# Loading queries and keys two tokens side by side in a partition, in an attention + two-MoE kernel

## The chip, the cores and the metric

The kernel runs on 1 core of one Trainium2 chip. The metric is the device time of one execution in microseconds (us), the median of several runs. The engines are named as in the profile: PE is the matmul engine (TensorE), PEld its weight loads, DVE is VectorE, ACT is ScalarE, POOL is GpSimd, and SP is the engine whose queue issues the DMAs here.

## What is computed

Windowed attention with a distance bias, then a soft mixture of experts, then a second mixture whose gate is balanced eight times. The change lies in the attention alone: how q and k get into the layout that the score matmul needs.

```python
# q, k, v: 4 batches x 8 heads x 576 tokens x 64, f32; window 128
scores = (q @ k.T) / 8 + slope[h] * -(i - j)      where 0 <= i - j < 128, else -1e9
attn   = softmax(scores);  x = (attn @ v) -> 2304 x 512
x = moe(x, phi, w1, w2)            # 8 experts, 4 slots each, 512 -> 1024 -> 512
x = moe2(x, w_gate, m1, m2)        # all 8 experts on every row; gate P from 8 rounds of row/column sums
```

## The kernel before, in words

**Stages.** The attention runs from the start to about 163 us. The soft mixture (`mm1`, line 764, and the loop at 839) runs to about 213 us. The second mixture, with its long row of f16 matmuls (lines 962 and 1034), fills the rest. Weights come in over SP's queue in all stages: during the attention the eight `w1` (`load_part`, line 57, 512 KB pieces) and `w2` of expert 0.

**Half-steps.** The attention works on two batches at a time (`j` = 0, 1) and on chunks of 64 queries, 9 chunks to a batch pair: 18 *tokens* `t` in the kernel's words. Each `t` is done in two half-steps of four heads, `s = 2 t + hf`, 36 in all. One trip of the loop at line 469 emits for half-step `s`: the DMAs, the scores of `s` (`emit_qk`, PE, then `emit_sm` on DVE), the normalization of `s-1` (`emit_nm`, DVE), the transposes of the weights of `s-2` (`emit_pt`, PE, copied out by ACT), the exponentials of `s` (`emit_exp`, ACT), the transposes that turn the next q and k (`emit_tr`), and the weighted sum of v for `s-3` (`emit_pv`, PE). `turned` then adds the transposes of a finished chunk (`emit_x`), and after every fourth chunk a generator (`group`, line 339) does the logits of the soft mixture, a piece per half-step. The schedule is manual: each engine and SP's queue run in the order in which the program emits.

**q and k.** `load_nat(t)` (line 126) loads chunk `t` of k and of q, two chunks ahead, into one tile each: 64 tokens of batch `j` = 0 on partitions 0 to 63, those of `j` = 1 on 64 to 127. One contiguous run in DRAM is one token of one head, 64 floats, 256 bytes. The second batch has neighbouring heads exchanged, so it takes two DMAs; a chunk takes six. The tiles have two buffers each. `emit_tr(t, "k")` makes four 128x128 transposes into one PSUM tile (pool `ps_t`, three buffers) in the first half-step of `t-1`, and DVE copies them into `kT` (line 156), a ring of four chunks; ACT copies some a second time (line 158) so that a window that wraps is contiguous. `emit_tr(t, "q")` makes two transposes in each half-step and DVE copies them into `qT` (line 160).

**Buffers that the change touches.** `xn` (line 273) holds up to five turned chunks for the sums of a group; `lt` and `lg` (lines 345 and 354) are small tiles of a group.

Of the kernel before, what the change touches and what calls it, by code (L numbers as in the profile page):

```python
# [8 lines left out]
F32 = mybir.dt.float32  # L9
# [15 lines left out]
def tile_kernel(ctx: ExitStack, tc: tile.TileContext, q, k, v, phi, w1, w2, w_gate, m1, m2, rel, out):  # L25
# [69 lines left out]
    with tc.manual_schedule():  # L95
        with ExitStack() as ab:
# [5 lines left out]
            with ExitStack() as at:  # L102
                nat = at.enter_context(tc.tile_pool(name="nat", bufs=2))
# [17 lines left out]
                qT = one.tile([128, 4, 2, 64], F32, name="qT")  # L121
# [4 lines left out]
                def load_nat(t):  # L126
                    bp, c = divmod(t, NCH)
                    for nm, src in (("k", k), ("q", q)):
                        nt_ = nat.tile([128, H, D], F32, tag=nm + "n", name=nm + "n")
                        nc.sync.dma_start(out=nt_[0:CH], in_=src[2 * bp, :, CH * c:CH * c + CH, :].rearrange("h i d -> i h d"))  # L130
                        heads = src[2 * bp + 1, :, CH * c:CH * c + CH, :].rearrange("(g a) i d -> i g a d", a=2)
                        turned_ = nt_[CH:].rearrange("p (g a) d -> p g a d", a=2)
                        for a in range(2):
                            nc.sync.dma_start(out=turned_[:, :, 1 - a, :], in_=heads[:, :, a, :])
                        natt[nm, t] = nt_
# [11 lines left out]
                def emit_tr(t, nm, gs=range(4)):  # L147
                    src = natt[nm, t]
                    ps = ps_t.tile([128, 4, 128], F32, tag="pt", name="pt")
                    for i, g in enumerate(gs):  # L150
                        nc.tensor.transpose(
                            ps[:, i, :], src[:, 2 * g:2 * g + 2, :].rearrange("p a d -> p (a d)"), idn)
                    pv_ = ps[:, 0:len(gs), :].rearrange("p g (j i) -> p g j i", j=2)
                    if nm == "k":
                        sl_ = t % 4
                        nc.vector.tensor_copy(out=kT[:, :, :, CH * sl_:CH * sl_ + CH], in_=pv_)
                        if sl_ < 2 and t >= 4:
                            nc.scalar.copy(out=kT[:, :, :, CH * (sl_ + 4):CH * (sl_ + 5)], in_=pv_)
                    else:
                        nc.vector.tensor_copy(out=qT[:, gs[0]:gs[-1] + 1], in_=pv_)  # L160
# [8 lines left out]
                def emit_qk(s):  # L169
                    t, hf = divmod(s, 2)  # L170
                    c = t % NCH
                    nch = min(c, 2) + 1
                    k0 = CH * ((t - nch + 1) % 4)
                    k1 = k0 + CH * nch
                    col = 192 - (k1 - k0)

                    ps = [ps_s.tile([128, 2, 256], F32, tag="s", name="s") for _ in range(2)]
                    for gg in range(2):
                        g = 2 * hf + gg
                        for j in range(2):  # L180
                            for a in range(2):
                                r0, c0 = CH * (a ^ j), CH * a
                                nc.tensor.matmul(ps[j][c0:c0 + CH, gg, col:192], lhsT=qT[r0:r0 + CH, g, j, :],  # L183
                                                 rhs=kT[r0:r0 + CH, g, j, k0:k1], start=True, stop=True,
                                                 tile_position=(r0, c0))
                    sc[s] = (ps, col)
# [82 lines left out]
                def emit_x(t):  # L269
# [3 lines left out]
                    xn[t] = sp.tile([128, DM], F32, tag="xn", name="xn", bufs=5)  # L273
# [65 lines left out]
                def group(g):  # L339
# [14 lines left out]
                    lg = sp.tile([128, 128], F32, tag="lg", name="lg", bufs=1)  # L354
# [20 lines left out]
                def group_end():  # L375
# [16 lines left out]
                    lg = sp.tile([128, 128], F32, tag="lg", name="lg", bufs=1)  # L392
# [40 lines left out]
                load_nat(0)  # L433
                nc.sync.dma_start(out=rel_sb[:, 3, :], in_=rel)
                load_nat(1)
# [5 lines left out]
                emit_tr(0, "k")  # L441
# [3 lines left out]
                emit_tr(0, "q", range(0, 2))  # L445
                emit_tr(0, "q", range(2, 4))

                NST = 2 * NT
                pre = [("w1", e, (wraw, wraw, wone, wpre, wpre, wpre, wpre, wcv)[e], p, 4) for e in range(NPRE) for p in range(4)]
# [8 lines left out]
                def turned():  # L458
                    while px:
                        t3 = px.pop(0)  # L460
                        if t3 < NT - 1:
                            emit_x(t3)
                        if t3 == NT - 1:
                            side.append(group_end())
                        elif t3 % 4 == 3:
                            side.append(group(t3 // 4))

                s = 0
                while s < NST + 4 or side or px:
                    t, hf = divmod(s, 2)  # L470
                    if s < NST:
                        if hf == 0:
# [12 lines left out]
                    if s < NST:  # L485
                        emit_exp(s)
                        if t + 1 < NT and hf == 0:
                            emit_tr(t + 1, "k")
                    if 3 <= s and s - 3 < NST:
                        emit_pv(s - 3)  # L490
                    if s < NST and t + 1 < NT:
                        emit_tr(t + 1, "q", range(2 * hf, 2 * hf + 2))
                    turned()
                    if 3 <= s and s - 3 < NST:
                        t3, hf3 = divmod(s - 3, 2)
                        if hf3 == 1:
                            emit_xt(t3)
                            px.append(t3)
# [730 lines left out]
```

## Time and profile before

| | |
|---|---|
| time, median of 3 runs | 973.59 us (971.21 to 976.7) |
| profiled execution, its own time | 977.32 us |
| its span, first to last instruction | 975.5 us |
| PE busy in the span | 940.9 us (96%) |
| DVE, ACT, POOL busy | 741.7, 611.8, 540.2 us |
| DMA packets under 512 B | 64240 of 95077 |

The span is the profiled time less 1.8 us around it. The profile counts an engine as busy while an instruction runs on it; a wait shows as the idle time in front of an instruction, with the one that ended it. In a timeline row the first number is the start, the second the length, both in us; `xN` means N instructions merged into one row; f32 matmuls count twice there. A timeline on SP shows the issue of a DMA, not its landing.

### The profile page before, as it was taken

The numbers are of one execution on the slowest core, as the hardware profiler recorded it, in microseconds if no ns is written. First come the engines' busy times: TensorE is split into PE (matmuls) and PEld (weight loads), VectorE is DVE, ScalarE is ACT, GpSimd is POOL, SyncE is SP. The second block draws the span as 40 slices with busy tenths as digits, with TensorE's granted clock in tenths as the row PEclk, the third lists the DMA queues.
The fourth block names the chain that finished last, engine by engine and source line by source line (L and its number), as shares of the span: only waits on it lengthen the run. The fifth ranks groups of instructions, "written<-read, shape, count | busy, mean of one in ns | idle before, by whom it ended". The sixth has DMA issues, their size and how long they took to land.

```text
span 975.5 us, 24588 instructions
## 1 busy us (share of the span) xinstructions
PE 940.9 (96%) x9629; PEld 790.9 (81%) x9629; DVE 741.7 (76%) x1920; ACT 611.8 (63%) x1493; POOL 540.2 (55%) x620
## 2 busy tenths in 40 slices
PE   8999999979899999999999999999999999999997
PEld 6676666437788888888888888888888888888886
DVE  5898886675996787777777777877787778777775
ACT  4777764646577677766666665666476656664442
POOL 0000000213488569857893897498658956995442
PEclk7999999999999999999999999999999999999999
DMA  6999999980200220032004001300220020001212
GB/s 132 241 236 227 237 269 329 365 311 2 98 2 1 94 92 2 1 101 85 1 2 164 22 1 57 129 2 2 89 97 1 2 94 6 1 2 34 55 44 66
DMA packets 95077, 90.13 MB, mean 92 GB/s; under 512 B 64240, under 2 KB 68208, under 8 KB 94960
## 3 DMA queue, kind: packets, MB, share of 16 engines
q1 hardware_dynamic: 94960, 88.55, 31.8%
q8 instruction: 76, 1.25, 0.5%
q14 instruction: 41, 0.34, 0.1%
HBM read 81.97 MB, written 4.72 MB: 89 GB/s over the span
## 4 chain that ended last, share of the span: by engine, by line
PE 69%; DVE 0%; issue 0%
PE x L1034 35%; PE y L1034 27%; PE z L962 6%; PE m L667 1%; PE m L542 0%; DVE ops L975 0%; DVE acc L1048 0%; DVE acc L1046 0%; PE m L925 0%
## 5 line engine op out<-in xcount | busy, mean ns | idle before, releaser
L1034 PEld LDWEIGHTS <-ops 128*128 128x128 f16 x6048 | 592.2, 98 | 73.8 <-issue 1.5
L994 POOL TENSOR_TENSOR ops<-s,ops 128x512 f16<-128x512 f32 x287 | 332.5, 1160 | 228.4 <-ACT ops L991 227.0
L1034 PE MATMUL x<-w2h,ops 128*128 128x256 f16 x2304 | 413.6, 273 | 2.2 <-ACT ops L972 0.7
L1034 PE MATMUL y<-w2h,ops 128*128 128x256 f16 x1728 | 319.5, 273 | 0.4 <-ACT ops L991 0.2
L1034 PE MATMUL x<-w2l,ops 128*128 128x256 f16 x1152 | 313.6, 273 | 0.0
L991 ACT CAST ops<-s 128x512 f16<-128x512 f32 x288 | 177.7, 617 | 216.0 <-DVE s L987 213.9
L1034 PE MATMUL y<-w2l,ops 128*128 128x256 f16 x864 | 235.6, 273 | 0.0
L1048 DVE SCALAR_TENSOR_TENSOR acc<-x,pe,acc 128x256 f32<-128x256 f32 x252 | 121.7, 483 | 77.5 <-PE x L1034 76.1
L972 ACT ACTIVATE ops<-z 128x512 f16<-128x512 f32 x216 | 128.6, 596 | 35.7 <-PE z L962 33.2
L975 DVE SCALAR_TENSOR_TENSOR ops<-z,ops 128x512 f16<-128x512 f32 x216 | 146.9, 680 | 0.0
L1048 DVE SCALAR_TENSOR_TENSOR acc<-y,pe,acc 128x256 f32<-128x256 f32 x189 | 91.3, 483 | 58.3 <-PE y L1034 57.9
L625 POOL TENSOR_TENSOR w2l<-w,w2h 128x256 f16<-128x256 f32 x168 | 112.7, 675 | 0.0
L987 DVE SCALAR_TENSOR_TENSOR s<-z,r 128x512 f32<-128x512 f32 x144 | 98.2, 682 | 11.3 <-ACT r L983 7.2
L987 DVE SCALAR_TENSOR_TENSOR s<-z,s 128x512 f32<-128x512 f32 x144 | 98.2, 682 | 6.5 <-ACT ops L972 6.3
L962 PE MATMUL z<-ct,stk 128*128 128x256 f16 x576 | 86.3, 273 | 4.5 <-DVE ops L975 3.8
L758 POOL MEMSET hz<- 128x480 f32 x2 | 1.0, 498 | 159.6 <-PE xp L258 158.4
L628 ACT CAST w2h<-w 128x256 f16<-128x256 f32 x168 | 67.3, 401 | 0.1
L962 PEld LDWEIGHTS <-stk 128*128 128x128 f16 x576 | 55.5, 98 | 14.3 <-DVE ops L975 4.8
L212 ACT ACTIVATE et<-et,mx 128x192 f32<-128x192 f32 (+2 forms) x144 | 61.2, 433 | 3.5 <-DVE mx L203 3.5
L203 DVE CUSTOM_DVE_ANT_0 et<-s,rel_sb 128x192 f32<-128x192 f32 (+2 forms) x144 | 39.5, 331 | 10.3 <-PE s L183 10.2
L258 PE MATMUL xp<-ptt,v 64*64 64x64 f32 (+1 forms) x1024 | 45.5, 244 | 1.5 <-DVE cn L328 0.5
L234 ACT COPY ptt<-pt 128x384 f32<-128x384 f32 (+2 forms) x72 | 28.6, 445 | 28.7 <-PE pt L233 28.6
(191 smaller groups left out, 917.7 us busy)
## 6 DMA issues: line engine op xcount, KB each, us to landing
w<-in_moe_w_dram SPq DMA_DIRECT2D x68, 512.0 KB, 7.3
w<-in_moe_w_dram SPq DMA_DIRECT2D x14, 2048.0 KB, 8.3
v<-in_v_dram SPq DMA_DIRECT2D x18, 256.0 KB, 4.8
out_dram<-acc SPq DMA_DIRECT2D x34, 128.0 KB, 2.4
kn<-in_k_dram SPq DMA_DIRECT2D x18, 128.0 KB, 6.2
kn<-in_k_dram SPq DMA_DIRECT2D x36, 64.0 KB, 5.3
qn<-in_q_dram SPq DMA_DIRECT2D x18, 128.0 KB, 5.4
qn<-in_q_dram SPq DMA_DIRECT2D x36, 64.0 KB, 4.8
```

The costliest lines, as they stand in the source:

```text
L212: nc.scalar.activation(out=runs[hh], in_=runs[hh], func=AF.Exp, bias=mx[:, hh:hh + 1], scale=-1.0, accum_out=sm[:, hh:hh + 1])
L258: nc.tensor.matmul(xp[j][64 * a:64 * a + 64, g, :], lhsT=vt[bp, vc, j][r0:r1, 2 * g + a, :], rhs=ptt[r0:r1, gg, 128 * blk + 64 * a:128 * b ...
L625: nc.gpsimd.tensor_tensor(out=out_, in0=x_, in1=y_, op=ALU.subtract)
L628: nc.scalar.copy(out=hi[:, i, r], in_=src[:, r])
L962: nc.tensor.matmul(ps[:, i], lhsT=stk[e][:, 128 * ft:128 * ft + 128], rhs=ct.rearrange("p (a n) t -> p a n t", a=2)[:, :, n, :], start=Tru ...
L972: nc.scalar.activation(out=ops_[m][:, k_, 0], in_=zb(m, i, j), func=AF.Relu)
L975: nc.vector.scalar_tensor_tensor(out=ops_[m][:, k_, 1], in0=zb(m, i, j), scalar=0.0, in1=ops_[m][:, k_, 0], op0=ALU.max, op1=ALU.subtract)
L987: nc.vector.scalar_tensor_tensor(out=new_sum(m, nm), in0=zb(m, i, j), scalar=0.0, in1=o, op0=ALU.max, op1=op)
L991: nc.scalar.copy(out=ops_[m][:, k_, 0], in_=sm_[m, nm])
L994: eng.tensor_tensor(out=ops_[m][:, k_, 1], in0=sm_[m, nm], in1=ops_[m][:, k_, 0], op=ALU.subtract)
L1034: nc.tensor.matmul(out_, lhsT=a_[:, k_, l_, i, :], rhs=r_[:, k_, i, :], start=(first and j == 0), stop=(j == 11), skip_group_check=True)
L1048: nc.vector.scalar_tensor_tensor(out=o, in0=ps, scalar=pe_[e][:, t:t + 1], in1=o, op0=ALU.mult, op1=ALU.add)
```

## The change

A *unit* is two neighbouring chunks of a batch pair (one chunk at the end, as there are nine), ten units in all. A tile now holds one unit's 128 tokens of both batches for four heads: partition `p` has tokens `2p` and `2p+1` side by side, so one contiguous run in DRAM is two tokens of one head, 128 floats, 512 bytes. After the landing, POOL exchanges the two middle blocks of 64 columns through a tile `swap` with three copies, so that a block of 128 columns holds one token of two heads. Four transposes turn a tile; the copies into `kT` and `qT` then write every second column. `qT` holds both chunks of a unit. q and k share one tag with four buffers, the tiles of one unit. `w1` comes in 1 MB pieces in every second half-step. `xn` has four buffers, and every fourth chunk is turned a half-step later; `lg` takes the buffer of `lt`.

```diff
-                nat = at.enter_context(tc.tile_pool(name="nat", bufs=2))
+                nat = at.enter_context(tc.tile_pool(name="nat", bufs=4))
-                qT = one.tile([128, 4, 2, 64], F32, name="qT")
+                qT = one.tile([128, 4, 2, 2 * CH], F32, name="qT")
+                swap = one.tile([128, 2, D], F32, name="swap")
-                def load_nat(t):
-                    bp, c = divmod(t, NCH)
-                    for nm, src in (("k", k), ("q", q)):
-                        nt_ = nat.tile([128, H, D], F32, tag=nm + "n", name=nm + "n")
...
+                units = [(bp, c, min(2, NCH - c)) for bp in range(2) for c in range(0, NCH, 2)]
+                wanted = [(u, nm, hf) for u in range(len(units)) for hf in range(2) for nm in "kq"]
+                def load_nat():
+                    if not wanted:
+                        return
+                    u, nm, hf = wanted.pop(0)
+                    bp, c, n = units[u]
+                    src = {"k": k, "q": q}[nm]
+                    nt_ = nat.tile([128, 2, 4, D], F32, tag="n", name=nm + "n")
+                    r1 = 32 * n
+                    for j in range(2):
+                        rows = nt_[r1 * j:r1 * j + r1].rearrange("p g (x r) d -> p g x (r d)", r=2)
+                        heads = src[2 * bp + j, 4 * hf:4 * hf + 4, CH * c:CH * (c + n), :].rearrange(
+                            "(g x) (p r) d -> p g x (r d)", x=2, r=2)
+                        if j == 0:
+                            nc.sync.dma_start(out=rows.rearrange("p g x e -> p (g x) e"),
+                                              in_=heads.rearrange("p g x e -> p (g x) e"))
+                        else:
+                            for x in range(2):
+                                nc.sync.dma_start(out=rows[:, :, 1 - x, :], in_=heads[:, :, x, :])
+                    all_ = nt_[0:2 * r1]
+                    nc.gpsimd.tensor_copy(out=swap[0:2 * r1], in_=all_[:, :, 1, :])
+                    nc.gpsimd.tensor_copy(out=all_[:, :, 1, :], in_=all_[:, :, 2, :])
+                    nc.gpsimd.tensor_copy(out=all_[:, :, 2, :], in_=swap[0:2 * r1])
+                    natt[u, nm, hf] = nt_
...
+                def emit_tr(u, nm, hf):
+                    bp, c, n = units[u]
+                    w = CH * n
+                    src = natt.pop((u, nm, hf))
+                    ps = ps_t.tile([128, 512], F32, tag="pt", name="pt")
+                    for i in range(4):
+                        r, g = divmod(i, 2)
+                        nc.tensor.transpose(ps[:, w * i:w * i + w],
+                                            src[0:w, g, 2 * r:2 * r + 2, :].rearrange("p x d -> p (x d)"), idn[0:w, 0:w])
+                    pv_ = ps[:, 0:4 * w].rearrange("q (r m p) -> q r m p", r=2, p=w // 2)
+                    def place(x_, o):
+                        return x_[:, 2 * hf:2 * hf + 2, :, o:o + w].rearrange("q g j (p r) -> q r (g j) p", r=2)
                     if nm == "k":
+                        nc.vector.tensor_copy(out=place(kT, CH * (c % 4)), in_=pv_)
+                        if c and c % 4 == 0:
+                            nc.scalar.copy(out=place(kT, CH * 4), in_=pv_)
                     else:
+                        nc.vector.tensor_copy(out=place(qT, 0), in_=pv_)
...
-                    xn[t] = sp.tile([128, DM], F32, tag="xn", name="xn", bufs=5)
+                    xn[t] = sp.tile([128, DM], F32, tag="xn", name="xn", bufs=4)
-                    lg = sp.tile([128, 128], F32, tag="lg", name="lg", bufs=1)
+                    lg = sp.tile([128, 128], F32, tag="lt", name="lg", bufs=1)
...
-                emit_tr(0, "q", range(0, 2))
-                emit_tr(0, "q", range(2, 4))
+                emit_tr(0, "q", 0)
+                for _ in range(2):
+                    load_nat()
+                for nm in "kq":
+                    emit_tr(0, nm, 1)
+                for _ in range(2):
+                    load_nat()
...
-                        if hf == 0:
-                            if t + 2 < NT:
-                                load_nat(t + 2)
-                        if s > 2 and pre:
+                        if s > 2 and s % 2 and pre:
                             load_part(*pre.pop(0))
...
-                        if t + 1 < NT and hf == 0:
-                            emit_tr(t + 1, "k")
+                        u = next((i for i, x_ in enumerate(units) if NCH * x_[0] + x_[1] == t + 1), None)
+                        if u is not None:
+                            emit_tr(u, "k", hf)
...
-                    if s < NST and t + 1 < NT:
-                        emit_tr(t + 1, "q", range(2 * hf, 2 * hf + 2))
+                    if s < NST and u is not None:
+                        emit_tr(u, "q", hf)
+                        for _ in range(2):
+                            load_nat()
...
-                            px.append(t3)
+                            px.append((s + 2 * (t3 % 4 == 0), t3))
```

**What moves on PE at the start of the program.** `pt<-idn,kn` and `pt<-idn,qn` are the transposes of k and q, `s<-kT,qT` the scores, eight to a half-step. Before (lines 151, 183):

```order
L83 MATMUL warm<-idn 128x128 x8
L151 MATMUL pt<-idn,kn 128x128 x4
L83 MATMUL warm<-idn 128x128 x3
L151 MATMUL pt<-idn,qn 128x128 x4
L183 MATMUL s<-kT,qT 64x64 x8
L151 MATMUL pt<-idn,kn 128x128 x4
L151 MATMUL pt<-idn,qn 128x128 x2
L183 MATMUL s<-kT,qT 64x64 x8
```

Changed (174 is the transpose, 210 the scores):

```order
L83 MATMUL warm<-idn 128x128 x8
L174 MATMUL pt<-idn,kn 128x128 x4
L83 MATMUL warm<-idn 128x128 x3
L174 MATMUL pt<-idn,qn 128x128 x4
L174 MATMUL pt<-idn,kn 128x128 x4
L174 MATMUL pt<-idn,qn 128x128 x4
L210 MATMUL s<-kT,qT 64x64 x16
L210 MATMUL s<-kT,qT 64x128 x8
```

The first scores now stand behind all four tiles of the first unit, where they stood behind one chunk of k and of q.

**What moves on SP's queue, from the first v to the first w1.** 130, 134 are loads of k and q, 144 of v, 64 of w1. Before:

```order
L144 DMA v<-in_v_dram 128x8x64
L144 DMA v<-in_v_dram 64x8x64
L130 DMA kn<-in_k_dram 64x8x64
L134 DMA kn<-in_k_dram 64x4x64 x2
L130 DMA qn<-in_q_dram 64x8x64
L134 DMA qn<-in_q_dram 64x4x64 x2
L144 DMA v<-in_v_dram 128x8x64 x3
L64 DMA w<-in_moe_w_dram 128x1024
```

Changed, from the loads of the second unit on (146, 150 are k and q, 164 is v):

```order
L146 DMA kn<-in_k_dram 64x4x128
L150 DMA kn<-in_k_dram 64x2x128 x2
L146 DMA qn<-in_q_dram 64x4x128
L150 DMA qn<-in_q_dram 64x2x128 x2
L146 DMA kn<-in_k_dram 64x4x128
L150 DMA kn<-in_k_dram 64x2x128 x2
L146 DMA qn<-in_q_dram 64x4x128
L150 DMA qn<-in_q_dram 64x2x128 x2
L164 DMA v<-in_v_dram 128x8x64
L164 DMA v<-in_v_dram 64x8x64
```

The first v stood behind 18 loads of k and q and now stands behind 24, and its rows are 64 floats long as before.

**What POOL gets.** In the attention POOL had nothing between two memsets. Before:

```order
masks.py:199 AFFINE_SELECT idn<-idn 128x128
L432 MEMSET ones 128x128
L382 MEMSET cn 128x64
L758 MEMSET hz_3069 128x480
L758 MEMSET hz_3070 128x480
```

Changed:

```order
masks.py:199 AFFINE_SELECT idn<-idn 128x128
L459 MEMSET ones 128x128
L152 COPY swap<-kn 128x128
L153 COPY kn<-kn 128x2x64
L154 COPY kn<-swap 128x2x64
L152 COPY swap<-qn 128x128
```

There are 40 tiles, so 120 such copies, each group of three ahead of the transposes of its tile.

## Rows read from the trace of the kernel before

**Rows 1.** The page, parts 1 and 2: PE's share, DMA share in 40 slices

```profile
PE 940.9 (96%) x9629; PEld 790.9 (81%) x9629; DVE 741.7 (76%) x1920; ACT 611.8 (63%) x1493; POOL 540.2 (55%) x620
...
DMA  6999999980200220032004001300220020001212
```

**Rows 2.** Busy time by stretch: length, engines, PE clock, DMA share, GB/s

```profile
37.00:99.00 62.00, 60.15 (x993) 44.34 (x996) 55.42 (x281) 47.10 (x181) 0.00 (x0) 1.00 1.05 234
...
163.00:213.00 50.00, 43.39 (x502) 20.83 (x502) 34.58 (x113) 25.47 (x77) 8.73 (x14) 1.00 0.91 331
```

**Rows 3.** Timeline of PE around its longest waits in the attention

```profile
32.86 0.41 PE L151 MATMUL pt<-idn,qn 128*128 128x128 f32 x2 [1.27 <-ACT kT L158]
...
64.80 1.06 PE L320 MATMUL ps<-xn,lg 128*32 128x512 f32 x8
...
98.69 0.88 PE L183 MATMUL s<-kT,qT 64*64 64x192 f32 x16
...
102.81 0.90 PE L151 MATMUL pt<-idn,kn 128*128 128x128 f32 x4 [2.25 <-ACT et L212]
...
105.31 1.40 PE L183 MATMUL s<-kT,qT 64*64 64x192 f32 x16
...
125.73 0.88 PE L183 MATMUL s<-kT,qT 64*64 64x192 f32 x16
...
129.62 0.63 PE L151 MATMUL pt<-idn,kn 128*128 128x128 f32 x4 [1.74 <-DVE et L222]
...
134.24 0.88 PE L183 MATMUL s<-kT,qT 64*64 64x192 f32 x16
...
137.97 0.88 PE L183 MATMUL s<-kT,qT 64*64 64x192 f32 x16
...
150.79 1.00 PE L258 MATMUL xp<-ptt,v 64*64 64x64 f32 x24 [0.51 <-DMA v<-in_v_dram]
```

**Rows 4.** Timeline of SP: issue of the k that PE took at 102.81

```profile
97.28 1.29 SPq L134 DMA_DIRECT2D kn<-in_k_dram  x2
```

**Rows 5.** The tile kn, all its loads: issue to landing

```profile
DMA to landing us min/median/max: 2.4/5.7/9.7
```

**Rows 6.** DMA queue, 0 to 12 us: packets, MB, share of 16 engines

```profile
q1 hardware_dynamic: 5468, 1.23, 47.7%
```

**Rows 7.** Timelines at the start: PE, and SP's first v

```profile
11.50 0.66 PE L151 MATMUL pt<-idn,qn 128*128 128x128 f32 x2 [1.04 <-DMA qn<-in_q_dram]
...
19.31 0.89 PE L258 MATMUL xp<-ptt,v 64*64 64x64 f32 x16
...
14.80 1.25 SPq L144 DMA_DIRECT2D v<-in_v_dram  x2
```

**Rows 8.** The tile v, all its loads: issue to landing

```profile
DMA to landing us min/median/max: 3.7/5.0/8.6
```

**Rows 9.** Groups by line and shape, 0 to 235 us: busy us, mean ns

```profile
L222 DVE TENSOR_SCALAR et<-et,rc 128x192 f32<-128x192 f32 x112 | 28.2, 316 | 1.0
...
L160 DVE COPY qT<-pt 128x256 f32<-128x256 f32 x36 | 15.0, 419 | 6.7 <-PE pt L151 6.6
...
L151 PE MATMUL pt<-idn,kn 128*128 128x128 f32 x72 | 12.7, 305 | 6.2 <-ACT et L212 2.3 <-DVE et L222 1.7 <-DMA kn<-in_k_dram 1.2
L156 DVE COPY kT<-pt 128x512 f32<-128x512 f32 x18 | 12.4, 686 | 6.0 <-PE pt L151 6.0
...
L222 DVE TENSOR_SCALAR et<-et,rc 128x64 f32<-128x64 f32 x16 | 3.0, 250 | 0.1
```

**Rows 10.** Timelines of POOL and of DVE in the soft mixture

```profile
175.31 0.21 POOL L835 COPY hz<-hT 128x32 f32<-128x32 f32 x1 [0.40 <-DVE hT L780]
...
190.37 1.48 POOL L600 TENSOR_TENSOR w<-w 128x512 f32<-128x512 f32 x1
...
190.23 2.69 DVE L584 SCALAR_TENSOR_TENSOR w2l<-w,w2i,w2h 128x256 f16<-128x256 f32 x4
...
199.25 1.66 DVE L584 SCALAR_TENSOR_TENSOR w2l<-w,w2i,w2h 128x256 f16<-128x256 f32 x4
```

More of the change, by code (lines that the diff above doesn't have):

```diff
@@ L172, in emit_qk @@
                     nch = min(c, 2) + 1
-                    k0 = CH * ((t - nch + 1) % 4)
+                    k0 = CH * ((c - nch + 1) % 4)
+                    q0 = CH * (c % 2)
                     k1 = k0 + CH * nch
@@ L391, in group_end @@
                     nc.tensor.matmul(psm[:, 0, :], lhsT=ones, rhs=dg, start=True, stop=True)
-                    lg = sp.tile([128, 128], F32, tag="lg", name="lg", bufs=1)
+                    lg = sp.tile([128, 128], F32, tag="lt", name="lg", bufs=1)
                     mm = sp.tile([128, NS], F32, name="mm", bufs=1)
@@ L444, in tile_kernel @@
                     nc.scalar.mul(rel_sb[:, g, :], rel_sb[:, 3, :], -(2.0 ** (2 - 2 * g)))
-                emit_tr(0, "q", range(0, 2))
-                emit_tr(0, "q", range(2, 4))
+                emit_tr(0, "q", 0)
[3 more added lines that the diff above has]
+                    emit_tr(0, nm, 1)
+                for _ in range(2):
+                    load_nat()
                 NST = 2 * NT
-                pre = [("w1", e, (wraw, wraw, wone, wpre, wpre, wpre, wpre, wcv)[e], p, 4) for e in range(NPRE) for p in range(4)]
+                pre = [("w1", e, (wraw, wraw, wone, wpre, wpre, wpre, wpre, wcv)[e], p, 2) for e in range(NPRE) for p in range(2)]
                 def load_w2_0(lo, hi):
@@ L458, in turned @@
                 def turned():
-                    while px:
-                        t3 = px.pop(0)
+                    while px and px[0][0] <= s:
+                        t3 = px.pop(0)[1]
                         if t3 < NT - 1:
@@ L486, in tile_kernel @@
                         emit_exp(s)
-                        if t + 1 < NT and hf == 0:
-                            emit_tr(t + 1, "k")
+                        u = next((i for i, x_ in enumerate(units) if NCH * x_[0] + x_[1] == t + 1), None)
+                        if u is not None:
+                            emit_tr(u, "k", hf)
                     if 3 <= s and s - 3 < NST:
                         emit_pv(s - 3)
-                    if s < NST and t + 1 < NT:
-                        emit_tr(t + 1, "q", range(2 * hf, 2 * hf + 2))
+                    if s < NST and u is not None:
+                        emit_tr(u, "q", hf)
+                        for _ in range(2):
+                            load_nat()
                     turned()
```

24 lines of the change are left out of this document (2 added, 22 removed).

## The prediction

> **What bounds the kernel now.** I read the page first: PE is busy in 96% of the span, and the DMA engines are nearly full in the slices from 24 to about 220 us and mostly idle after that [rows 1]. The change touches DMAs in the first stretch only, so I went to the stretches. In the steady attention PE is busy for 60.15 of 62.00 us at full clock, DVE for 55.42, and the DMA share is 1.05 [rows 2]. PE, DVE and the DMA engines are thus all close to full, with PE ahead; what a lighter DMA can give is only what PE waits for it. In the soft mixture behind it the DMA share is 0.91 and PE has 6.6 us idle in 50 [rows 2]; the weights there are issued when buffers come free of earlier work, so I take that stage, and the main one behind it, as shifted and not shortened.
>
> Where PE waits for loads in the attention is read from its timeline [rows 3]. A plain half-step is 137.97 - 134.24 = 3.73 us. The one from 98.69 to 105.31 took 6.62: PE stood for 2.25 us before the transposes of k. The profile names an exponential as the releaser, but that had long been due; the k in question was still being issued until 98.6 us [rows 4], and a load of k lands 5.7 us after its issue in the median, 9.7 at most [rows 5]. The half-step from 125.73 to 134.24 took 8.51, of which 1.06 are the sums of a group; again PE stood before k, for 1.74 us, and its matmuls then ran at half pace for some microseconds (eight score matmuls took 1.40 us at 105.31 behind the other wait, against 0.88). So late loads cost 6.62 - 3.73 = 2.9 and 8.51 - 3.73 - 1.06 = 3.7 us. Smaller ones: 1.27 us before q at 32.86, and 0.51 for v at 150.79.
>
> **The change part by part.** All terms are against the profiled execution.
>
> *Late loads.* k and q are 2 x 4 x 8 x 576 rows of 256 B, 36,864 packets; they become 18,432 of 512 B. At the start, where DMA is not full, 5,468 packets of mostly 256 B took 47.7% of 12 us on 16 engines, 16.7 ns each [rows 6]. No row has a 512 B packet in bulk: if it costs the same, 18,432 x 16.7 ns / 16 = 19 us of engine time go away; if twice as much, nothing. The Trainium skill (DMA: Bandwidth & Descriptors, section Specifications) gives 512 B as the smallest transfer at line rate; by that the 19 us would go, an estimate. The sum does not hang on it, because the loads also move ahead: a unit's four tiles have four buffers, and each is asked for as soon as the same tile of the unit before is turned, four half-steps or 15 us before it is needed, against a largest landing time of 9.7 [rows 5]. Both readings remove the waits before k and q: -2.9 - 3.7 - 1.3. I leave half of the 0.51 for v, whose packets stay: -0.3. Together **-8.2**; at worst half of it, -4.1.
>
> *One short lead.* The last unit of a batch pair is one chunk, so the next unit has two half-steps, 7.5 us, less than issue (2 us for a tile's three DMAs), 5.7 us of landing and POOL's copies together. **+0.5**, between 0 and 2.
>
> *The start.* The first scores wait for the last tile of the first unit. Its loads are issued where chunk 1 was, whose q PE took at 11.50 [rows 7], and POOL's copies and two more sets of transposes come on top; then half-steps 0 to 3 need nothing new but the second unit. The first v decides: it was issued at 14.80 [rows 7] and now stands behind six more loads, about 0.65 us each, so at 18.6. With the shortest landing of a v, 3.7 us [rows 8], the first weighted sum moves from 19.31 to 22.3: **+3.0**. It is +1 if halving the packets speeds these landings, +5.5 if the delay of the first scores (11.50 + 1 + 1 = 13.5 against 8) stays whole.
>
> *PE's transposes.* 144 of 128 columns become 128 of them and 32 of 64 columns. By the 12.7 us of 72 [rows 9] one is 0.18; the 32 narrow ones are worth between 16 and 32 full ones, so 0 to +2.8. I take **+1.0**.
>
> *Evictions.* DVE had 18 x 0.686 + 36 x 0.419 = 27.4 us [rows 9] and gets 32 x 0.686 + 8 x 0.419 = 25.3. Written to every second column they may be slower: no row shows that. 256 columns more cost such a copy 267 ns, 1.04 ns a column, twice what line 222 pays (below), so it is not in a fast form that it could lose, and I take the same rate; the other end is half rate, a rival below. Zero on the path: DVE has 6.6 us idle in 62 [rows 2]. ACT's second copies are fewer or narrower, and ACT is idle a quarter of that stretch. Both evictions now fall into the half-steps of odd chunks, but PE's transposes do too.
>
> *POOL's copies.* 120 of 128 columns. A POOL copy of 32 columns took 0.21 us, a subtraction of 512 columns 1.48 [rows 10]; I take 0.3 us, nearest the copy, 36 us in all, on an engine that was idle. They are not free for DVE, though. Four `L584` took 1.66 us alone and 2.69 with the POOL subtraction of 1.48 beside them [rows 10], so DVE lost 0.7 of POOL's time. In the attention the DVE operation that could lose is the scaling of line 222: 128 columns more cost it 66 ns, 0.52 ns a column [rows 9]. It runs 28.2 + 3.0 us and some 3.5 for the middle width, 35 us of the 150 or so in which it runs at all. By chance overlap DVE loses 36 x 35/150 x 0.7 = 6 us, against 6.6/62 of 150, some 16 us, of DVE idle time [rows 2]. **+1.5** on the path, between 0 and 6. The Trainium skill (SBUF — State Buffer, section SBUF: two separate sides) states such a rule: DVE in a two-port mode and GpSimd lock each other out for a whole instruction. The rows agree for `L584`; no row shows it for line 222.
>
> *The rest.* SP issues 120 loads of k and q for 108, and 16 pieces of w1 for 32: nobody waits for SP then. A load behind a 1 MB piece lands later; the lead of 15 us covers it. `xn` with four buffers would make ACT wait for the sums of a group, and the later turn covers that; without it, one half-step in four would lose a part of its 1.06 us. `lg` in `lt`'s place waits for readers that are done a half-step earlier.
>
> Sum: -8.2 + 0.5 + 3.0 + 1.0 + 1.5 = **-2.2 us**, 977.32 to 975.1. The profiled execution lies 3.7 us above the median of 973.59; I carry the difference over: **971.4**. If that run was long because it had more late loads than the others, less is to be had.
>
> **The rivals.** About 0.5%, 4.9 us, is what a measurement here can tell from no change.
>
> *A: the lighter DMA gives more.* With half the packets the start is +1, DVE and POOL don't meet, the turn costs nothing and the narrow transposes half: -8.2 + 1 = -7.2, and the remaining 1.9 us of PE idle time in 62 [rows 2] go too: -9, so 964.5 to 966.5. For it: a DMA share of 1.05 in the whole stretch. Against it: PE is at 97% there. Chance 0.34.
>
> *B: POOL takes DVE's place in the queue.* If a tile's three copies mostly meet line 222, DVE loses up to 36 x 0.7 = 25 us; it has 16 to give, so from 0.13 us a copy on (16/120) DVE becomes the bound: 9 us in place of 1.5, so +5.3, 979; more with bad timing. Against it: copies run when a load lands, at no fixed place in the half-step. Chance 0.11.
>
> *C: writing every second column halves the eviction rate.* 32 x 0.53 + 8 x 0.27 = 19 us more on DVE, 3 more than its idle time, and in pairs: +6, so +4, 977.5. Chance 0.06.
>
> *D: the loads are still late.* 1 MB pieces in the way, three copies more before each tile: the 8.2 stay: +6, 979.6. Against it the lead of 15 us. Chance 0.07.
>
> **How the numbers follow.** My forecast has 0.42, its own range 966.5 to 976. Faster by over 0.5% is A and a little of the forecast's range, 0.36; slower is B, D and half of C, 0.21; the rest, 0.43, is within. The range of 963 to 980 takes in A and the near parts of B, C and D, and leaves out some 0.15.
>
> **What would show it.** Right: no idle time of over a microsecond on PE before a transpose of k or q behind 40 us; PE's clock full from 30 us to the end of the attention; the first weighted sum near 22 us; `L222`'s successor in groups of little over 1.01 us; evictions of 686 ns; about 36 us on POOL; soft mixture and main stage as long as before. Wrong: evictions of a microsecond or more (C), scalings stretched and PE waiting for DVE (B), waits before k or q still there (D), or an attention shorter by over 7 us (A).

## Result and the profile after the change

The changed kernel took 979.45 us in the median of 10 runs (976.85 to 982.34) against 974.08 for the kernel before (971.21 to 976.70): a ratio of 1.0055, 95% interval 1.0038 to 1.0072. It is 5.4 us slower; 971.4 had been forecast.

The two profiled executions do not show this at once: the one before took 977.32 us, more than any of its ten runs, and the one after 976.99, at the lower end of its own. Read side by side they are equal, so each point below also leans on profiles of the variants.

The page after, parts 1 and 2:

```profile
PE 940.1 (96%) x9645; PEld 790.7 (81%) x9645; DVE 742.6 (76%) x1906; ACT 611.4 (63%) x1493; POOL 576.3 (59%) x740
...
DMA  4989988980200220031005001300220020001222
```

Against [rows 1], PE has the same work, POOL 36 us more, and the DMA engines are less full. The stretches of [rows 2] after the change:

```profile
37.00:99.00 62.00, 57.95 (x961) 42.72 (x959) 54.18 (x259) 43.94 (x168) 17.01 (x57) 1.00 0.89 234
163.00:213.00 50.00, 43.67 (x500) 20.99 (x500) 34.11 (x113) 25.66 (x77) 8.22 (x12) 1.00 0.88 324
```

The DMA share fell from 1.05 to 0.89 in the steady attention, yet PE is busy for 57.95 of 62 us where it was 60.15: it waits more in this stretch, with lighter DMA; the two long waits of before lie outside it. PE's waits, from its timeline (start, length, and in brackets the idle time before it and what ended that):

```profile
23.20 0.48 PE L285 MATMUL xp<-ptt,v 64*64 64x64 f32 x4 [1.87 <-DMA v<-in_v_dram]
...
53.10 0.80 PE L174 MATMUL pt<-idn,kn 128*128 128x128 f32 x4 [0.73 <-POOL kn L153]
...
80.46 0.80 PE L174 MATMUL pt<-idn,kn 128*128 128x128 f32 x4 [1.19 <-DVE rc L247]
...
96.08 0.63 PE L174 MATMUL pt<-idn,kn 128*128 128x128 f32 x4 [1.61 <-DMA kn<-in_k_dram]
...
110.44 0.55 PE L260 MATMUL pt<-idn,et 128*128 128x128 f32 x3 [1.17 <-ACT kT L184]
...
128.13 0.63 PE L174 MATMUL pt<-idn,kn 128*128 128x128 f32 x4 [0.94 <-DMA kn<-in_k_dram]
...
149.55 0.83 PE L210 MATMUL s<-kT,qT 64*64 64x192 f32 x16
```

The two long waits of [rows 3] have become five shorter ones. Only those at 53.10 and 80.46 are for a load, whatever the brackets say: the k of 96.08, put down to its load, was on POOL by 89.77 (row below), and what PE waited for there and at 128.13 stands under 4. At 110.44 it is ScalarE's second copy of k, which has its like before. The scores of the last half-step, the last row here, began at 148.26 us in the profile before. Groups by shape, 0 to 235 us (busy us, mean ns), answering [rows 9]:

```profile
L249 DVE TENSOR_SCALAR et<-et,rc 128x192 f32<-128x192 f32 x112 | 30.5, 335 | 1.0
...
L186 DVE COPY qT<-pt 128x512 f32<-128x512 f32 x16 | 11.0, 687 | 6.6 <-PE pt L174 6.6
L182 DVE COPY kT<-pt 128x512 f32<-128x512 f32 x16 | 10.9, 681 | 6.0 <-PE pt L174 6.0
```

An eviction into every second column takes 681 to 687 ns, as one into neighbouring columns did (686). The scalings of 128x192 grew from 316 to 335 ns. And the tile kn, all its loads, from issue to landing, where [rows 5] had 2.4/5.7/9.7:

```profile
DMA to landing us min/median/max: 2.2/5.3/8.9
```

So the loads became little faster. Three of them, the k of 53.10, of 80.46 and of 96.08, in the timelines of PE, SP and POOL:

```profile
37.37 0.80 PE L174 MATMUL pt<-idn,kn 128*128 128x128 f32 x4
...
42.66 0.60 SPq L146 DMA_DIRECT2D kn<-in_k_dram  x1
43.31 2.20 SPq L150 DMA_DIRECT2D kn<-in_k_dram  x2
...
52.39 0.30 POOL L152 COPY swap<-kn 128x128 f32<-128x128 f32 x1 [8.09 <-DMA kn<-in_k_dram]
...
71.71 1.39 SPq L146 DMA_DIRECT2D kn<-in_k_dram  x1
73.14 1.27 SPq L150 DMA_DIRECT2D kn<-in_k_dram  x2
...
79.75 0.30 POOL L152 COPY swap<-kn 128x128 f32<-128x128 f32 x1 [7.14 <-DMA kn<-in_k_dram]
...
89.77 0.30 POOL L152 COPY swap<-kn 128x128 f32<-128x128 f32 x1 [3.11 <-DMA kn<-in_k_dram]
```

The k of 53.10 got its buffer with the turn at 37.37, was asked for from 42.66 to 45.51 us, and POOL could copy it at 52.39. The k of 80.46 was asked for from 71.71 to 74.41 us, POOL could copy at 79.75, and PE waited for it until 80.46.

### The profile page after: what moved, and what is told of

It is laid out like the page before. It is cut to its first block, busy times and chain, and to the rows that moved or that the text cites. A ratio compares the mean times of both kernels' runs of the same rounds, so it can differ in the third digit from the quotient of the medians.

```text
span 975.2 us, 24852 instructions
## 1 busy us (share of the span) xinstructions
PE 940.1 (96%) x9645; PEld 790.7 (81%) x9645; DVE 742.6 (76%) x1906; ACT 611.4 (63%) x1493; POOL 576.3 (59%) x740
## 3 DMA queue, kind: packets, MB, share of 16 engines
q1 hardware_dynamic: 76464, 88.55, 29.3%
## 4 chain that ended last, share of the span: by engine, by line
PE 69%; DVE 0%; issue 0%
PE x L1069 35%; PE y L1069 27%; PE z L997 6%; PE m L702 1%; PE m L577 0%; DVE ops L1010 0%; DVE acc L1083 0%; DVE acc L1081 0%; PE m L960 0%
## 5 line engine op out<-in xcount | busy, mean ns | idle before, releaser
L152 POOL COPY swap<-kn 128x128 f32<-128x128 f32 (+1 forms) x20 | 5.9, 294 | 87.0 <-DMA kn<-in_k_dram 87.0
L285 PEld LDWEIGHTS xp<-ptt,v 64*64 64x64 f32 (+1 forms) x1024 | 33.4, 136 | 13.8 <-issue 3.4
```

The source lines that it names most:

```text
L285: nc.tensor.matmul(xp[j][64 * a:64 * a + 64, g, :], lhsT=vt[bp, vc, j][r0:r1, 2 * g + a, :], rhs=ptt[r0:r1, gg, 128 * blk + 64 * a:128 * b ...
```

## Experiments

Ratios are to the kernel before, run on the same chip; the change itself stands at 1.0055. The time of a profiled execution scatters by some 3 us, so that small steps are read from stretches of its trace.

**1. The start, and SP's order.** First theory: the start costs 4 us because v stands on SP behind the second unit's loads, and k and q of a second half-step are late because they stand behind v and w1. Run e1_start:

```
 emit_tr(0, "q", 0)
+load_v(0, 0)
+load_v(0, -1)
 for _ in range(2): load_nat()
-for nm in "kq": emit_tr(0, nm, 1)
-for _ in range(2): load_nat()
...
 emit_exp(s)
+if s == 0:
+    for nm in "kq": emit_tr(0, nm, 1)
+    for _ in range(2): load_nat()
...
-if c == 0:
+if c == 0 and bp:
     load_v(bp, 0)
```

> The changed kernel with another start: both first loads of v stand on SP right behind the turn of the first half of the first unit, ahead of the second unit's loads, and the turns of the unit's second half stand behind the first scores. Theory 1 (late loads: the start costs some 4 us, and in the attention k and q of a second half-step stand on SP behind v and 1 MB of w1): first weighted sum back from 23.2 to about 20 us, time 3 to 4.5 us less than the change, about 975.5. Theory 2 (GpSimd's copies): the first three copies of two tiles still stand ahead, 1 us or less gained, 978.5. Theory 3 (the 1 MB pieces): the start does not hang on them, the same 3 us as by theory 1.

981.18 us, ratio 1.006 (1.004 to 1.0081): no gain. The first weighted sum came at 22.82 us although the first scores came at 9.12 (after: 12.79). No wait of over 0.8 us is left between 13 and 28 us; PE is simply busy there at half clock (granted 0.50 from 15 to 25 us, the 1.2 GHz level, after PE had been idle for 2.3 of the 5 us from 10 to 15), where a tile's four transposes take 1.1 us and not 0.6.

Run e2_k1_first: w1 and the next v behind the loads of k and q in odd half-steps.

```
-if s > 2 and s % 2 and pre: load_part(*pre.pop(0))
...
     for _ in range(2): load_nat()
+if s < NST and s > 2 and s % 2 and pre: load_part(*pre.pop(0))
+if s < NST and hf and (t % NCH) % 2: load_v(t // NCH, t % NCH + 1)
...
-load_v(bp, c + 1)
```

> The changed kernel with another order on SP alone: in an odd half-step the piece of w1 is issued behind the pair of k and q and no longer ahead of it, and the v of the next chunk moves from the even half-step to the odd one, behind that pair too. Theory 1: the waits of PE before a k of a second half-step (0.73, 1.19, 1.61 and 0.94 us in the profile of the change, with the slower clock behind some of them in other executions) go, time 3 to 6 us less than the change, 974 to 976. Theory 2: nothing, 979.5. Theory 3 (a 1 MB piece in the way on the DMA engines wherever it stands): at most 1 us, 978.5.

980.74 us, 1.0056 (1.0035 to 1.0078). No k is late any more (two waits before k remain, of 1.46 and 0.85 us, which have another cause, under 4); PE now waits for v, 4.8 us in six places behind 30 us. Run e4_start_k1 is both edits:

> The start of the first run and the order on SP of the second, together. Theory 1: the sum of both, 6 to 10 us less than the change, 969.5 to 973.5, faster than the kernel before too. Theory 2: 1 us, 978.5. Theory 3: about 3 us, that of the start alone, 976.5.

980.20 us, 1.0052 (1.0037 to 1.0067). The first theory fell: another order decides which load is late, not how much time is lost.

**2. GpSimd's copies.** Run e3_no_swap drops the three `nc.gpsimd.tensor_copy` of `load_nat`, so that the heads stay in the order of the load.

> The changed kernel without GpSimd's three copies of each tile, so that the blocks of heads stand unswapped and the output is another than the reference's. Theory 2: DVE's scalings of 128x192 go back from 335 to 316 ns and each tile is ready 1 us earlier; if that is what the change lost, 4 to 5 us less than the change, about 975. Theory 1: about 1 us at the start and some tenths at each late load, 1.5 to 3 us less, 977 to 978. Theory 3: 1 us, 978.5.

978.26 us, 1.0035 (1.0018 to 1.0051), 0.002 or 2 us below the change, with intervals that overlap: a part of the loss at most. DVE's scalings, in this run's groups, are back where they were before:

```profile
L246 DVE TENSOR_SCALAR et<-et,rc 128x192 f32<-128x192 f32 x112 | 28.2, 316 | 1.0
```

**3. Was the profile before an unlucky one?** Run b2_before_again is the kernel before, once more.

> The kernel before, unchanged, for a second profiled execution. Theory A (the profiled execution of before was an unlucky one: its two waits of 2.25 and 1.74 us before k are mostly absent from others, so what the change could win was never 8.2 us): a time near 974, one or none of these waits, and the first weight matmul of the soft mixture at about 164 us and not at 167.4. Theory B (the late loads are in every execution, and the change loses them elsewhere): both waits again and 167 us, with the time again near 977.

974.51 us, with the first weight matmul at 165.35. PE's waits for k in it:

```profile
31.22 0.63 PE L151 MATMUL pt<-idn,kn 128*128 128x128 f32 x4 [2.67 <-DMA kn<-in_k_dram]
...
102.75 0.63 PE L151 MATMUL pt<-idn,kn 128*128 128x128 f32 x4 [1.14 <-DMA kn<-in_k_dram]
...
128.07 0.63 PE L151 MATMUL pt<-idn,kn 128*128 128x128 f32 x4 [1.47 <-DMA kn<-in_k_dram]
```

The waits are at the places of [rows 3], one longer and two shorter. Theory A fell: the late loads are in this execution too, which took little more than the median, and there was something to win.

**4. Bunched turns.** A unit's four turns stand in two half-steps and share three PSUM buffers. Run x1_spread sets them in three half-steps:

```
-emit_tr(u, "k", hf) ... emit_tr(u, "q", hf)
+hf 0: emit_tr(u, "k", 0)
+hf 1: emit_tr(u, "q", 0) ... emit_tr(u, "k", 1)
+hf 0 of the unit itself, behind emit_pv: emit_tr(u0, "q", 1)
```

> The changed kernel with the turns of a unit spread over three half-steps (k of the first half, then q of the first half and k of the second, then q of the second) in place of two and two, each load behind the turn that frees its buffer. Theory A (start and lost lottery): the spread does little, 1 us either way, 978.5 to 980.5. Theory C (the four turns in two half-steps fill the three PSUM buffers that they share with the exponentials' turns, and PE waits there): the waits of PE at about 96, 110 and 128 us, some 3.5 us, mostly go, 976. Theory D (1 MB pieces in the way): no change.

984.00 us, 1.0091 (1.007 to 1.0111). The last turn now stood just ahead of the scores that need it: PE waits for DVE's copy of q there, 5.1 us in nine places. The edit brought a wait of its own and says nothing on the bunching; behind 96 us the turn of q, now in k's place, still waits 1.32 us, for what is found next.

Run x2_kT_from_sbuf:

```
-nc.scalar.copy(out=place(kT, CH * 4), in_=pv_)
+nc.scalar.copy(out=kT[..., CH * 4:CH * 4 + w], in_=kT[..., 0:w])
```

> The changed kernel with ScalarE's second copy of k taken from kT in SBUF and no longer from the PSUM tile, so that the tile is free as soon as DVE has copied it. Theory C: PE's wait for that copy (1.17 us at 110 us, 0.31 at 36 us) goes, 1 to 1.5 us less than the change, 978. Theories A and D: the wait goes and another takes its place, within 0.5 us of the change, 979 to 980.

979.77 us, 1.0047 (1.0031 to 1.0062): the wait at 110 us shrank from 1.17 to 0.44 us, and the time stayed.

Every profile of the changed kernel with its usual order of turns and groups has a wait of 1.35 to 1.61 us before a k between 92 and 101 us. Where no load is late there, as in e4_start_k1, DVE's copies, ScalarE and PE show what makes it:

```profile
90.65 0.68 DVE L182 COPY kT<-pt 128x512 f32<-128x512 f32 x1
...
91.10 0.27 PE L341 MATMUL pt<-idn,lt 128*128 128x128 f32 x1
...
91.30 0.69 DVE L186 COPY qT<-pt 128x512 f32<-128x512 f32 x1
...
93.33 0.29 DVE L355 TENSOR_TENSOR cn<-pt,rm 128x128 f32<-128x128 f32 x1
...
93.78 0.41 ACT L261 COPY ptt<-pt 128x128 f32<-128x128 f32 x2
...
93.84 0.63 PE L174 MATMUL pt<-idn,kn 128*128 128x128 f32 x4 [1.46 <-issue]
```

PE turns the group's logits `lt` at 91.10 into one of the three PSUM buffers of `ps_t`; DVE copies k and q first, then does the group's maxima and reads the turned logits last, at 93.33 (`cn<-pt`). The k is the third tile behind them and needs their buffer: PE takes it 0.22 us after that read ends. It does not wait for ScalarE's copies of the exponentials' turns, as the expectation below has it, for these begin at 93.78 and still run when PE starts. In the profiles with this wait, and in the change's own at 96.08 and 128.13, the turn comes 0.1 to 0.4 us behind that read, whatever the bracket names. The kernel before has a shorter wait for the same read, here in y2_before_no_w1 (under 6): its second half-steps turn no k, and its q stands behind a weighted sum.

```profile
89.96 0.41 PE L151 MATMUL pt<-idn,qn 128*128 128x128 f32 x2 [0.62 <-DVE cn L328]
```

Run x5_group_later moves the rest of two groups behind it:

```
 nc.scalar.copy(out=lt, in_=ps[:, 0, :])
-yield
+for _ in range(3 if g else 1): yield
...
-px.append((s + 2 * (t3 % 4 == 0), t3))
+px.append((s + (2 if t3 < 8 else 4) * (t3 % 4 == 0), t3))
```

> The changed kernel with the second and the third group's maxima, turns and sums two half-steps later (their logits where they were), in half-steps without turns of k and q. Theory C2 (in half-steps with two turns DVE copies out k and q, 1.37 us, ahead of the group's maxima, ScalarE waits for these with the copies of the exponentials' turns queued behind, and PE waits for their PSUM buffers): the waits of 1.46 us at 96 and 0.85 to 1.1 us at 128 us, which every profile of the changed kernel so far has, go, 2 to 3 us less than the change, 977. Against it: they move to other half-steps, within 1 us of the change.

985.17 us, 1.0118 (1.0086 to 1.0149). Both waits went; others came, of 0.81 us for the scalings and 1.40 for ScalarE's copy of k, at 103 and 111 us. Run x7_combined has all four edits:

> The start of the first run, the order on SP of the second, ScalarE's copy of k from SBUF and the later groups, together. Each alone did nothing or is not known; if the waits are independent and each only hidden by the next, together 4 to 6 us less than the change, 974 to 976; if one cause behind them sets the pace (theory E, the weights' traffic), 978 to 980 as before.

983.04 us, 1.0092 (1.0069 to 1.0116). No order of the same work that was tried is clearly better than the change's own.

**5. The pieces of w1.** Run x3_half_pieces undoes them in the changed kernel (`p, 4) ... range(4)`, and `if s > 2 and pre`); z4_before_big_pieces makes only this part of the change in the kernel before.

> The changed kernel with w1 loaded as before, 512 KB in every half-step and not 1 MB in every second one. Theory D (a 1 MB piece in the way of a load of k, q or v): PE's waits for loads at 53, 80, 96 and 128 us shrink, 2 to 4 us less than the change, 976 to 977. Theories A and C: within 1 us of the change, 978.5 to 980.5.

> The kernel before with one part of the change alone: w1 in pieces of 1 MB in every second half-step and not 512 KB in every one. If the larger pieces cost the change its gain, 2 to 5 us slower than before, 977 to 980; if not (undoing them in the changed kernel gave no gain), within 1 us of before, 974 to 976.

981.87 us, 1.0063 (1.0039 to 1.0088), and 975.31 us, 1.0002 (0.9988 to 1.0017): the size of the pieces is worth nothing that the runs can tell, either way. A single execution can mislead here: z4's profiled one, 977.05 us, has a wait of 6.79 us before the k of 36.64.

**6. The attention without w1.** Runs y1_change_no_w1 and y2_before_no_w1, the same edit in both:

```
-if s > 2 ... and pre: load_part(*pre.pop(0))
+if s > 31 ... and pre and pre[0][1] == 0: load_part(*pre.pop(0))
-if s in (26, 30): load_w2_0(...)
...
 while pre: load_part(*pre.pop(0))
+load_w2_0(0, 4)
+load_w2_0(4, FC)
```

> The changed kernel with all w1 but the first expert's, and the kept quarter of w2, issued behind the attention, so that k, q and v have the DMA engines nearly to themselves; only the attention is to be read, up to the scores of the last half-step (149.55 us in the profile of the change), since the soft mixture now waits for its weights. Theory E (the weights' traffic and their places on SP make the loads late, in both kernels, and behind that the changed attention is itself longer, by its start and by the half-steps in which four turns stand): no wait for k, q or v behind 30 us, last scores at 143 to 145. Theory F (the loads are late by their own lead, four buffers and SP's order): the waits stay, last scores at 148 to 150.

> The kernel before with the same loads issued behind the attention (last scores at 148.26 and 145.63 us in its two profiles). Theory E: its waits for k go too, last scores at 137 to 140, so 5 us or so ahead of the changed kernel under the same condition: that is what the change itself costs. Theory F: the waits stay, 145 to 148, and the two kernels then differ by 2 us or less.

The scores of the last half-step and the landing of kn, first the change, then the kernel before:

```profile
146.17 0.83 PE L210 MATMUL s<-kT,qT 64*64 64x192 f32 x16
...
DMA to landing us min/median/max: 1.7/2.7/4.9
```

```profile
142.49 0.83 PE L183 MATMUL s<-kT,qT 64*64 64x192 f32 x16
...
DMA to landing us min/median/max: 2.4/3.3/4.8
```

This pair decides most, though each of the two is one execution. Without the weights no load holds PE behind 30 us in the kernel before; in the changed one two waits remain at the places of the group's chain above (1.46 and 0.97 us), there with a load named as releaser. The changed attention is 3.7 us longer, where theory E had expected 5 or so: that is its own. With the weights the kernel before comes to 148.26 and 145.63, 5.8 and 3.1 us more, and the changed one to 149.55 in its low execution, 3.4 more. (e1_start and e2_k1_first, other orders of it, come to 153.59 and 153.54.) The start scatters from execution to execution, so I also count from the scores of half-step 6 to the last ones. Both rows in the profile before and in b2_before_again, and half-step 6 in y2_before_no_w1:

```profile
27.86 0.88 PE L183 MATMUL s<-kT,qT 64*64 64x192 f32 x16
...
148.26 0.83 PE L183 MATMUL s<-kT,qT 64*64 64x192 f32 x16
```

```profile
26.58 0.88 PE L183 MATMUL s<-kT,qT 64*64 64x192 f32 x16
...
145.63 0.83 PE L183 MATMUL s<-kT,qT 64*64 64x192 f32 x16
```

```profile
29.25 0.88 PE L183 MATMUL s<-kT,qT 64*64 64x192 f32 x16
```

Half-step 6 after the change and in y1_change_no_w1:

```profile
31.07 0.88 PE L210 MATMUL s<-kT,qT 64*64 64x192 f32 x16
```

```profile
30.77 0.88 PE L210 MATMUL s<-kT,qT 64*64 64x192 f32 x16
```

The kernel before takes 120.40 and 119.05 us with the weights and 113.24 without, 7.2 and 5.8 more; the changed one 118.48 in its low execution and 115.40 without, 3.1 more. Its median lies 2.5 us above that execution; if those fall into the attention (what follows the last scores took 829.1, 828.9 and 827.4 us in these three executions with the weights), the weights cost it some 5.5 in the usual run, an estimate. They thus cost about what they did before the packets were halved; only in the low execution is it some 3 to 4 us less.

**7. Where the weights are in the way.** Run z1_w1_on_pool_queue:

```
-load_part(*pre.pop(0))
+load_part(*pre.pop(0), q=nc.gpsimd)
```

> The changed kernel with w1's pieces in the attention issued on GpSimd's DMA queue and no longer on SP's. On SP every DMA waits until the one eight places ahead of it has landed; a unit's two half-steps issue 12 loads of k and q and up to 3 of v there, with a 1 MB piece among them. Theory G (SP's order: loads are late since they stand behind a piece that has not landed): SP's waits for w go, PE's waits for k, q and v mostly too, last scores near the 146.2 us of the run without w1, time 3 to 6 us less than the change, 974 to 976. Theory H (the DMA engines themselves: the weights' bytes are in the way wherever they are issued): the waits stay, within 1.5 us of the change, 978 to 981. GpSimd's own issue beside its copies may add a late copy or two.

985.85 us, 1.0121 (1.0101 to 1.0141). In the change SP waited 15.6 us for pieces of w1 (20 to 146 us); those waits are gone. PE's are not, and v lands later than the 4.1 us it took after the change (KB each, median us to landing, 30 to 150 us):

```profile
w<-in_moe_w_dram POOLq DMA_DIRECT2D x14, 1024.0 KB, 6.5
v<-in_v_dram SPq DMA_DIRECT2D x13, 256.0 KB, 6.6
```

Theory G, SP's order as the whole cause, fell; the weights' traffic slows the loads from the other queue too. That GpSimd's queue is of another kind (`software_dynamic` on its page, SP's is `hardware_dynamic`) and may cost something of its own was not separated, nor whether the traffic is in the way in the DMA engines or in memory.

Runs z2_change_w2_later and z3_before_w2_later put only the 2 MB of w2 behind the attention:

> The changed kernel with the 2 MB of w2 that it loads in half-steps 26 and 30 issued behind the attention. Theory G or H: fewer late loads in the last ten half-steps only, where the change has few, so 0 to 2 us less than the change, 978 to 979.5, unless the soft mixture then waits for its weights, which adds up to 7 us.

> The kernel before with the same 2 MB of w2 behind the attention. Its half-step 30 took 8.51 and 6.86 us in the two profiles, 3.1 to 4.8 more than the plain 3.73: if these 2 MB are the cause, 2 to 4 us less than before, 971 to 973, faster than both kernels; if the soft mixture then waits, no gain or some us more.

979.44 us, 1.0052 (1.0033 to 1.0071): nothing. The kernel before gained, at the edge of what the runs can tell: 972.76 us, 0.9982 (0.9965 to 0.9999). Its half-step from 125.73 to 134.24 [rows 3] now takes 5.19 us and not 8.51 (6.86 in b2_before_again):

```profile
128.18 0.88 PE L183 MATMUL s<-kT,qT 64*64 64x192 f32 x16
133.37 0.88 PE L183 MATMUL s<-kT,qT 64*64 64x192 f32 x16
```

This is the one version faster than both, some 2 us faster than the kernel before. More of it failed. Runs v1_before_less_early and v2_change_less_early also begin w1 at half-step 9 (`s > 8`):

> The kernel before with the 2 MB of w2 behind the attention, as in the run that gained 0.2%, and the first piece of w1 not in half-step 3 but in 9, so that 3 MB more come behind the attention. The weights' bytes are what makes k late (theory H): the wait of 1.9 to 2.7 us before k at 31 us goes as well, 1.5 to 3 us less than that run, 969.5 to 971.5, if the soft mixture still finds its weights in time; if it waits for them, 973 to 980.

> The changed kernel with the same two shifts of its weights. Theory H and a cost of the change's own of 3.7 us or more: this one gains 1 to 4 us on the change, 975.5 to 978.5, and stays 4 to 6 us behind the run beside it. If lighter weights let the change's loads be in time and the kernel before keeps its own late ones, the two come within 2 us of each other.

979.08 us, 1.0038 (1.0023 to 1.0052), and 987.13 us, 1.0121 (1.0102 to 1.014). The soft mixture of v1 now waits for weights, first ScalarE and behind it PE:

```profile
179.48 0.63 ACT L550 ACTIVATE t<-w 128x512 f32<-128x512 f32 x1 [6.77 <-DMA w<-in_moe_w_dram]
...
182.75 0.59 PE L808 MATMUL bc<-id,cs 128*128 128x128 f16 x4 [7.54 <-DVE hT L780]
```

The distance between the two kernels did not shrink (8.0 us).

## Why the prediction was wrong

**The step that failed: late loads, -8.2.** The prediction said that either price of a packet removes the waits, because each load is asked for "four half-steps or 15 us before it is needed, against a largest landing time of 9.7". Two things in this sentence did not hold. The 15 us are there from the freeing of the buffer to the need, but not from the asking: the k of 53.10 had its buffer from the turn at 37.37 on, and SP, which works through a unit's loads, v and w1 in order, came to it at 42.66, so that under 10 us were left. The prediction said of SP's issues that "nobody waits for SP then"; PE did. And landing hardly shortened (5.7 to 5.3 us in the median, 8.9 at most), because the weights are in flight beside these loads: without them it is 3.3 and 2.7 us. What was removed at the old places came back at new ones. Measured in place of -8.2: about zero in the usual run (5.8 and 7.2 us of loss before, 5.5 after, an estimate), -3 to -4 in the change's low execution. The outcome is that of rival D (979.6), which had 0.07, but D's reasons are not what the runs show: the pieces of 1 MB were worth nothing (5) and the copies 2 us at most (2). That its number is so near is luck, since the other terms were off too.

That the lighter packets free the engines was right: 18,496 fewer, and the queue's share went from 31.8% to 29.3% of the span, 310.2 - 285.7 = 24.5 us of engine time, where 19 had been estimated. The Trainium skill (DMA: Bandwidth & Descriptors, section Specifications), which gives 512 B as the smallest transfer at line rate, agrees with that; the time of the kernel did not follow it.

**The start, +3.0.** Mechanism partly, size right. With the same chunks turned, half-step 6 began at 27.86 and 26.58 us before and at 31.07 after, 3.2 to 4.5 later. The first weighted sum, forecast at 22.3, came at 23.20 behind 1.87 us of waiting for v. But e1_start shows that v alone does not bind: without that wait the sum still came at 22.82, behind work at half clock, and half-step 6 at 29.74. The clock was not in the sum. From 10 to 30 us it is granted at 0.66 in the mean in the profile before, at 0.83 in b2_before_again and at 0.66 after (the last figures but two; rows in this order):

```profile
10.00:30.00 20.00, 18.02 (x190) 11.82 (x189) 15.92 (x88) 12.02 (x55) 0.00 (x0) 0.66 0.88 178
```

```profile
10.00:30.00 20.00, 15.87 (x186) 10.24 (x186) 16.85 (x94) 13.12 (x59) 0.00 (x0) 0.83 0.89 181
```

```profile
10.00:30.00 20.00, 15.84 (x161) 10.64 (x161) 13.02 (x72) 9.09 (x45) 6.53 (x22) 0.66 0.65 149
```

Against the first, PE is busy 2.2 us less, so the change loses by waits; against the second it is as busy, at a lower clock. How the 3.2 to 4.5 us divide between the two stays open.

**Short lead, +0.5, between 0 and 2.** The place was right: the half-step behind the one-chunk unit took 5.94 us in the change's profile against 4.39 in the profiles where no load was late, so 1.6, within the range; in x2_kT_from_sbuf it took 8.45, 4.1 more.

**PE's turns, +1.0.** Sign wrong, little weight: 17.0 and 12.7 us of busy time for q and k became 11.7, 11.2, 1.8 and 1.8; two in a row took 0.44 us and four 0.60 to 0.66 at full clock.

**Evictions, 0.** Their rate was right, which ends rival C. Their place was not nothing: two wide ones ahead of a group's maxima stand in the chain under 4. It was dismissed because DVE is idle for a tenth of the time; the queue order mattered, not the share.

**POOL, +1.5.** Of the right size as far as can be told: the scalings lost 2.3 us of busy time, where 6 by chance overlap had been estimated, and it goes when the copies go; the whole kernel then gains 2 us, with overlapping intervals. Rival B is far off. The Trainium skill (SBUF — State Buffer, section SBUF: two separate sides) describes a lock that DVE, in a two-port mode, or GpSimd holds for a whole instruction while the other waits; the direction, 335 ns against 316, agrees with that, and no row shows DVE's mode or the lock itself.

**The rest.** Soft mixture and main stage are as long as before: 45.55 us from the first weight matmul to the first z against 45.66. The larger pieces cost nothing, as said.

Put together: the change's own cost is 3.7 us in the pair without weights. In that pair half-step 6 began at 29.25 and 30.77, only 1.5 apart; with the usual 3.2 to 4.5 at that place and the remaining 2.2, it would be 5.4 to 6.7, an estimate that fits the measured 5.4 with nothing won from the loads. Of the 2.2, the chain would be 1.8 by the lengths of its waits in the pair (1.46 and 0.97 against 0.62), again an estimate: no run settled it, since x1_spread and x5_group_later each brought waits of their own.

## What to carry to other kernels

A wait for a load is the difference of lead and landing; read both from the trace at the place, issue row and landing row, before crediting a lighter transfer with the whole wait, and ask what else is on the engines at that time. The releaser that a profile names can be wrong, as it was for the k of 96.08: look at when that load was in place. Leaving the competing traffic out, in both kernels, told what the changes of order had not: what the change itself costs. And work gathered into fewer, larger pieces needs a look at what stands behind it in each queue, even on an engine that is idle for a tenth of the time.

## What the runs showed that was not expected

- Moving w1 to GpSimd's queue made v, on SP's, land at 6.6 us instead of 4.1, and the kernel 6 us slower than the change.
- Copies into every second column cost DVE nothing extra (681 and 687 against 686 ns).
- Waits are not additive here: shortening one of 1.17 us to 0.44 (x2_kT_from_sbuf), or bringing k in time at the cost of v (e2_k1_first), left the time where it was.
